# Wide tile products moved between the narrow products of the rest, in a cluster attention and expert kernel

## The chip, the cores and the metric

The kernel runs on one core of one Trainium2 chip. The metric is the device time of one execution in microseconds. A core has TensorE (PE, matrix products into PSUM; its weight loads are shown apart as PEld), VectorE (DVE), ScalarE (ACT), GpSimd (POOL) and SyncE (SP, which issues most transfers). Each engine runs its own instruction stream in order and waits for the others by semaphores.

## The reference

Attention in which a query sees only the keys of its own cluster feeds a layer of 16 experts; every token goes to one expert, chosen by an argmax over 4 groups and then over 4 experts of the group.

```
mask   = argmax(q_n @ c_n)[:, :, :, None] == argmax(k_n @ c_n)[:, :, None, :]
attn   = softmax(where(mask, q @ k.T / 8, -1e9));  x = (attn @ v).reshape(3072, 512)
for g in range(4):
    for e in range(4):                      # tokens whose argmax is (g, e)
        h  = maximum(x[tok] @ w1[g, e], 0)  # w1: 512 x 1024
        ye = h @ w2[g, e]                   # w2: 1024 x 512
        out[tok] = (g_w * e_w)[:, None] * ye
```

Shapes: q, k, v are 4 x 8 x 768 x 64 in fp32, with 16 clusters a head.

## The kernel before

The first 400 us or so are the attention; the change leaves them as they are. Then the experts run, one after another. Each fp32 operand is split into a high and a low fp16 part, so that a product becomes three: high by high, low weights by high, high weights by low.

One expert (that with most tokens) is done first. The other 15 are sorted by their counts into ranks 0 to 14. Rank k has room for a fixed number of tokens, `caps[k]`: 288, 272, 256, 240, 232, 224, 216, 208, 200, 192, 184, 176, 168, 160, 160. A rank has a first product (x by w1, 96 matmuls: 8 blocks of 128 hidden features, 12 matmuls each) and a second product (h by w2). The second product has three forms:

- by tile: 128 tokens are the stationary operand and 512 output features stream past; 24 wide matmuls per tile of 128 tokens, and the tile is ready to be written out;
- turned (features by tokens, `all_features`, L1724): w2 is the stationary operand and the tokens stream past, 96 matmuls as wide as the tokens; the result is evicted as two fp16 parts (yh on ACT, yl on DVE), and `settle` (L1358) turns it back with 8 small products a tile;
- both: the first 128 tokens by tile (`tile_then`, L1714), the rest (`caps[k]` - 128 tokens: 112 down to 48) turned (`rest_first`, L1697). The function `both` decides it by column counts: ranks 3 to 11 take this form, ranks 12 to 14 are wholly turned, ranks 0 and 1 too, by the older function `down`; rank 2 goes by tile, also through `down`.

From rank 2 on, `phases` (L1604) writes the order out by hand. One turn k of its loop does, on PE: the first product of rank k; the transposes of the tokens of rank k+1; the second product of rank k-1, which for the form `both` is all 96 narrow matmuls of the rest, then `settle` of what rank k-2 owes, then the 24 wide ones of the tile. Between them `fills` puts pieces of the weight stream: each piece is one of 8 quarters (512 KB in fp32) of a rank's weights, loaded by SP, its high part made by ACT or POOL (the second argument of `fills` says which) and its low part by DVE (L1060). Six loads are under way at a time; a load waits for the DVE instruction that frees a staging buffer.

`sized` (L1585) wraps blocks of 12 matmuls in a branch: PE reads the rank's count, and takes a body that is 24 columns narrower if the count allows it (the first matmul of a block stays at full width). Both bodies stand in PE's program behind each other. Every product is pinned to the order as written.

PSUM has a pool of two banks for second products (psy), one of two banks for the small ones (psm), and four banks for first products (psh three, and one called psm, from the pool `fourth`). `emit` (L1370) scales a finished tile on ACT into one of three y buffers (L1372), and POOL scatters it to the output (L1374).

Of the kernel before, what the change touches and what calls it, by code (L numbers as in the profile page):

```python
# [13 lines left out]
F32 = mybir.dt.float32  # L14
# [8 lines left out]
P = 128  # L23
# [967 lines left out]
class Experts:  # L991
# [6 lines left out]
    short, eng = (), None  # L998
    AHEAD = 6
    SLT = 14  # L1000
    FILL, SETTLE, TOK = (0, 1, 2, 3, 4, 5, 6, 7), 2, 5
    HI = (0, 1, 0, 1, 0, 1, 0, 1)
    LEAD = 12
# [353 lines left out]
    def settle(self):  # L1357

        nc = self.nc
        while self.owed:  # L1360
            ys, M, gcols, idcols = self.owed.pop(0)
            for t, (g, idc) in enumerate(zip(gcols, idcols)):
                n = min(P, M - t * P)
                py = self.R.psm.tile([P, 512], F32, name="psm")
                for d in range(self.R.KD):
                    for i, y in enumerate(ys):
                        nc.tensor.matmul(out=py[:, d * P:(d + 1) * P], lhsT=y[:, d * M + t * P:d * M + (t + 1) * P], rhs=self.back, start=i == 0, stop=i == 1)
                self.emit(py, n, g, idc)
# [233 lines left out]
    def phases(self, first, xT, down, bg):  # L1602

        nc, tc, R, E = self.nc, self.tc, self.R, self.R.E  # L1604
        KD, FC, D = R.KD, self.F // P, self.D
        xgs = self.gathers(first + 1)
        _, self.counts = nc.values_load_multi_w_load_instructions(self.ei[0:1, E:2 * E - 1], engines=[ET.PE], skip_runtime_bounds_check_because="they are only compared with constants")
        R.psm = self.psm2
        h = None

        self.pinned, self.behind_of = (nc.cur_bb, len(nc.cur_bb.bb.instructions)), {}

        def fills(n, eng):
            self.eng = eng
            for _ in range(n):
                next(self.fill, None)

        for k in range(first, E):
            if k < E - 1:
                M = self.caps[k]  # L1620
                while self.ready < 4 * k + 4:
                    fills(1, 0)
                w1h, w1l = self.weights_of(k, 0)
                hp = [next(self.quads).tile([P, 512], F32, name="psh" if i < 3 else "psm").rearrange("p (a x) -> p a x", a=2) for i in range(4)]

                prods = [(w, x, c) for c in range(KD) for w, x in ((w1h, 0), (w1h, 1), (w1l, 0))]
                for f in range(FC):

                    def up(m):
                        for i, (w, x, c) in enumerate(prods):  # L1630
                            n = m if i else M
                            self.mm = nc.tensor.matmul(out=hp[f // 2][:, f % 2, 0:n], lhsT=w[:, c, f * P:(f + 1) * P], rhs=xT[:, x, c, 0:n], start=i == 0, stop=i == len(prods) - 1)  # L1632

                    self.sized(k, (24,), up)
                nh = [self.xp.tile([P, FC, M], F16, name=f"h{x}") for x in "hl"]
                for j, p in enumerate(hp):
                    fs = slice(2 * j, 2 * j + 2)
                    nc.scalar.activation(out=nh[0][:, fs], in_=p[:, :, 0:M], func=AF.Relu)  # L1638
                    nc.vector.scalar_tensor_tensor(out=nh[1][:, fs], in0=p[:, :, 0:M], scalar=0.0, in1=nh[0][:, fs], op0=ALU.max, op1=ALU.subtract)
            fills(2, 1)  # L1640
            if k < E - 2:
                nT = self.xp.tile([P, 2, KD, self.caps[k + 1]], F16, name="xT")
                for t, xg in enumerate(xgs):
                    self.transposed(nT, xg, t, min(P, nT.shape[3] - t * P), R.psm.tile([P, 512], F32, name="psm"), nc.scalar.copy)
                xgs = self.gathers(k + 2) if k < E - 3 else None
            fills(2, 0)
            while self.ready2 < 4 * (k - 1) + 4:
                fills(1, 0)
            m = self.caps[k - 1]
            due, self.owed = self.owed, []  # L1650
            if h is None or not (self.both(m) or self.feature_major(m)):
                down = down if h is None else self.down(h, m, self.weights_of(k - 1, 1), *self.columns_of(k - 1))
                for i, _ in enumerate(down):
                    if i == 1:
                        new, self.owed = self.owed, due
                        self.settle()
                        self.owed = new
                    if i in (2, 4, 6):
                        fills(1, i == 4)
                fills(1, 0)  # L1660
                next(bg, None)
            else:
                (self.rest_first if self.both(m) else self.all_features)(k - 1, m, h)
                fills(2, 1)
                if k == E - 2:
                    nc.gpsimd.drain()  # L1666
                new, self.owed = self.owed, due
                self.settle()
                self.owed = new
                fills(2, 0)  # L1670
                next(bg, None)
                if self.both(m):
                    self.tile_then(k - 1, h)
            if k < E - 1:
                h, xT = nh, nT if k < E - 2 else None
        for _ in self.fill:
            pass
        self.settle()
        self.pin()
# [12 lines left out]
    def products(self, h, W):  # L1692
        return [(w, a, f) for w, a in ((W[0], h[0]), (W[1], h[0]), (W[0], h[1])) for f in range(self.F // P)]

    def rest_first(self, k, M, h):

        nc, KD, n = self.nc, self.R.KD, M - P  # L1697
        prods = self.products(h, self.weights_of(k, 1))
        pr = self.ps_y.tile([P, 512], F32, name="psy")[:, 0:KD * n].rearrange("p (d m) -> p d m", m=n)

        for d in range(KD):
            for i, (w, a, f) in enumerate(prods):
                self.mm = nc.tensor.matmul(out=pr[:, d], lhsT=w[:, f, d * P:(d + 1) * P], rhs=a[:, f, P:M], start=i == 0, stop=i == len(prods) - 1)
        ys = [self.xp.tile([P, (KD - 1) * n + P], F16, name=f"y{x}") for x in "hl"]
        if n < P:
            for y in ys:
                nc.vector.memset(y[:, KD * n:], 0.0)
        yh, yl = (y[:, 0:KD * n].rearrange("p (d m) -> p d m", m=n) for y in ys)
        nc.scalar.activation(out=yh, in_=pr, func=AF.Copy, scale=1.0 / YS)
        self.ev = nc.vector.scalar_tensor_tensor(out=yl, in0=pr, scalar=1.0 / YS, in1=yh, op0=ALU.mult, op1=ALU.subtract)  # L1710
        g, ids = self.columns_of(k)
        self.owed.append((ys, n, g[1:], ids[1:]))

    def tile_then(self, k, h):  # L1714

        nc, D = self.nc, self.D
        prods = self.products(h, self.weights_of(k, 1))
        pt = self.ps_y.tile([P, 512], F32, name="psy")
        for i, (w, a, f) in enumerate(prods):
            self.mm = nc.tensor.matmul(out=pt, lhsT=a[:, f, 0:P], rhs=w[:, f], start=i == 0, stop=i == len(prods) - 1)  # L1720
        g, ids = self.columns_of(k)
        self.emit(pt, P, g[0], ids[0])

    def all_features(self, k, M, h):  # L1724

        nc, KD = self.nc, self.R.KD
        prods = self.products(h, self.weights_of(k, 1))
# [6 lines left out]
        for c in range(2):  # L1734
            py = self.ps_y.tile([P, 512], F32, name="psy").rearrange("p (a x) -> p a x", a=2)

            for j in range(2):
                d = 2 * c + j
# [10 lines left out]
            nc.scalar.activation(out=yh[:, ds], in_=py[:, :, 0:M], func=AF.Copy, scale=1.0 / YS)  # L1749
            self.ev = nc.vector.scalar_tensor_tensor(out=yl[:, ds], in0=py[:, :, 0:M], scalar=1.0 / YS, in1=yh[:, ds], op0=ALU.mult, op1=ALU.subtract)  # L1750
        self.owed.append((ys, M, *self.columns_of(k)))

    def rest(self):
        self.again = True
# [99 lines left out]
def tile_cluster_attention_moe(ctx, tc, qT, kT, vr, cen, wr, w1, w2, out):  # L1854
# [39 lines left out]
    for i, _ in enumerate(ga):  # L1894
        with tc.issue_after(X.mm.ins):
            if i == X.SLT:
                X.xTB = X.tokens([X.xB], P)
# [45 lines left out]
```

## Time and profile before

| | us |
|---|---|
| median of 3 runs (729.63 to 731.92) | 731.0 |
| the profiled execution | 729.34 |
| its span, first to last instruction | 727.3 |
| PE busy in the span | 698.2 (96%) |
| DVE, POOL, ACT busy | 585.7, 504.4, 487.8 |
| mean granted clock of PE, share of full speed | 0.993 |

The 2.0 us between the execution's time and its span lie outside of the first and the last instruction. A PE row's duration is longer than the distance from one matmul's start to the next, since matmuls overlap; the distance between starts is what a matmul costs in a stream. Idle time before a row stands in brackets with what ended it; "issue" means that the profile shows nothing that the engine waited for. DMA share is the mean busy share of the 16 DMA engines; queue q8 carries instructions.

### The profile page before, as it was taken

Reading aid. Unit: us, or ns where it says so; the run is one execution under the profiler, and the core shown is the slowest. Engines: PE = TensorE matmul, PEld = TensorE weight load, DVE = VectorE, ACT = ScalarE, POOL = GpSimd, SP = SyncE. Lnnn points to the kernel's source line nnn. Section 1 sums busy time; section 2 is a strip of 40 time slices with the busy share of each in tenths; the row PEclk is TensorE's granted clock in tenths of the full one; section 3 lists DMA queues with packets and bytes.
Section 4 is the critical chain, followed back from the end, with each engine's and each line's share of the span. In section 5 each row is a group of like instructions: output and inputs, shape, how many; then the busy total and the mean of one; then the engine's idle time right before and its main releaser. Section 6 shows DMA issues by size and latency. Waiting matters only on the chain. (4 is left out here: it accounts for less than half of the span.)

```text
span 727.3 us, 22864 instructions
## 1 busy us (share of the span) xinstructions
PE 698.2 (96%) x9035; PEld 578.8 (80%) x9035; DVE 585.7 (81%) x1202; ACT 487.8 (67%) x932; POOL 504.4 (69%) x522
## 2 busy tenths in 40 slices
PE   8899999999999999999999999999999999999984
PEld 4677888888888888888888877898788888877884
DVE  6898989899898998998888677556599798788742
ACT  6669987888878978787888366354445554565422
POOL 8799999897898988979896454313645444667433
PEclk9999999999999999999999999999999999999998
DMA  8735634516255262340430698626778776888721
GB/s 242 208 108 170 190 106 133 172 47 188 66 140 179 64 174 58 79 132 2 148 100 14 223 379 292 205 86 220 255 256 311 280 274 238 308 291 301 252 90 51
DMA packets 45813, 127.93 MB, mean 176 GB/s; under 512 B 7648, under 2 KB 12640, under 8 KB 45688
## 3 DMA queue, kind: packets, MB, share of 16 engines
q1 hardware_dynamic: 40668, 112.64, 48.1%
q0 software_dynamic: 4864, 13.54, 5.2%
q8 instruction: 85, 1.39, 0.8%
q14 instruction: 40, 0.33, 0.1%
q10 hardware_dynamic: 156, 0.03, 0.0%
HBM read 93.30 MB, written 13.54 MB: 147 GB/s over the span
## 5 line engine op out<-in xcount | busy, mean ns | idle before, releaser
L436 POOL TENSOR_TENSOR pl<-p 128x512 f16<-128x512 f32 x278 | 284.6, 1044 | 46.8 <-ACT p L434 43.5
L390 DVE TENSOR_REDUCE mpart<-psc 128x1 f32<-128x512 f32 (+1 forms) x282 | 190.5, 684 | 23.4 <-PE psc L387 22.2
L434 ACT ACTIVATE p<-psf 128x512 f32<-128x512 f32 x288 | 170.7, 599 | 39.6 <-PE psf L430 34.3
L454 PE MATMUL pso<-V,pl 128*128 128x129 f16 x1152 | 165.1, 219 | 0.8 <-POOL pl L436 0.8
L454 PE MATMUL pso<-V,p 128*128 128x129 f16 x1152 | 165.6, 219 | 0.0
L429 PE MATMUL psf<-A 82*128 82x384 f16 (+2 forms) x576 | 142.6, 273 | 3.1 <-ACT p L434 2.3
L430 PE MATMUL psf<-B 128*128 128x384 f16 (+2 forms) x576 | 143.4, 273 | 0.0
L454 PEld LDWEIGHTS <-pl 128*128 128x128 f16 x1152 | 112.0, 97 | 21.9 <-POOL pl L436 1.3
L1374 POOL DMA_INDIRECT out_dram<-y,ri x33 | 44.1, 1335 | 113.1 <-ACT y L1373 106.5
L454 PEld LDWEIGHTS <-p 128*128 128x128 bf16 x1152 | 112.2, 97 | 8.5
L387 PE MATMUL psc<-A 80*128 80x512 f16 (+1 forms) x376 | 106.6, 325 | 0.9 <-DVE A L335 0.5
L430 PEld LDWEIGHTS <-B 128*128 128x128 f16 x576 | 56.5, 98 | 14.7 <-issue 5.5
L429 PEld LDWEIGHTS <-A 82*128 82x128 f16 x576 | 56.0, 98 | 9.6 <-issue 1.1
L1638 ACT ACTIVATE hh<-psh 128x320 f16<-128x320 f32 (+11 forms) x39 | 19.7, 506 | 45.0 <-PE psh L1632 45.0
L1060 DVE SCALAR_TENSOR_TENSOR wl1b<-st,wh1b 128x1024 f16<-128x1024 f32 x32 | 44.6, 1425 | 3.2 <-ACT wh1b L1057 1.7
L1060 DVE SCALAR_TENSOR_TENSOR wl0a<-st,wh0a 128x1024 f16<-128x1024 f32 x32 | 41.1, 1310 | 4.9 <-ACT wh0a L1057 4.9
L1057 ACT ACTIVATE wh0a<-st 128x1024 f16<-128x1024 f32 x30 | 31.1, 1059 | 20.3 <-DMA st<-w 17.5
L1060 DVE SCALAR_TENSOR_TENSOR wl1a<-st,wh1a 128x1024 f16<-128x1024 f32 x28 | 37.3, 1363 | 8.9 <-POOL wh1a L1059 7.2
L387 PEld LDWEIGHTS <-A 80*128 80x128 f16 x384 | 36.2, 98 | 9.7 <-issue 0.8
L1234 POOL DMA_INDIRECT xg<-xbuf,ri x25 | 29.5, 1181 | 19.0 <-DVE rg L1389 8.8
L1632 PEld LDWEIGHTS <-wh0a 128*128 128x128 f16 x448 | 39.1, 98 | 4.2 <-issue 2.9
L1059 POOL TENSOR_SCALAR wh1a<-st 128x1024 f16<-128x1024 f32 x25 | 32.2, 1303 | 14.0 <-DMA st<-w 12.2
(455 smaller groups left out, 1699.7 us busy)
## 6 DMA issues: line engine op xcount, KB each, us to landing
st<-w SPq DMA_DIRECT2D x128, 512.0 KB
B<-parts SPq DMA_DIRECT2D x60, 192.0 KB
kx<-kT SPq DMA_DIRECT2D x16, 384.0 KB
qx<-qT SPq DMA_DIRECT2D x16, 384.0 KB
vx<-vr SPq DMA_DIRECT2D x16, 384.0 KB
xbuf<-xs SPq DMA_DIRECT2D x4, 1536.0 KB
A<-parts SPq DMA_DIRECT2D x30, 192.0 KB
A<-mk SPq DMA_DIRECT2D x56, 24.0 KB
```

The lines of the kernel that those rows point to most:

```text
L387: last["mm"] = nc.tensor.matmul(out=pc[:, off:off + k1 - k0], lhsT=QA[h % 8][0:80, c * P:(c + 1) * P], rhs=KA[h % 8][0:80, k0:k1], start=T ...
L390: nc.vector.tensor_reduce(out=(mp[:, 0, 0:1], mp[:, :, 1], mp[:, 1, 0:1])[i], in_=pc.rearrange("p (a x) -> p a x", a=n), axis=AX.X, op=ALU ...
L429: nc.tensor.matmul(out=o, lhsT=KA[h % 8][0:82, ks], rhs=QA[h % 8][0:82, q0:q1], start=True, stop=False)
L430: nc.tensor.matmul(out=o, lhsT=KBs[h][:, ks], rhs=QBs[h][:, q0:q1], start=False, stop=True)
L434: exps[9 * h + u] = cfg["exp"] = nc.scalar.activation(out=p32, in_=pf, func=AF.Exp, scale=QK / (SQ * SQ))
L436: lo = (nc.vector if u in (EARLY if h < 2 else DVE_LO[h % 8] if h < NH - 2 else DVE_END) else nc.gpsimd).tensor_tensor(out=pl, in0=p32, in ...
L454: nc.tensor.matmul(out=o, lhsT=p[:, bs], rhs=vv, start=c == 0 and q % HB == 0 and i == 0, stop=c == NCH - 1 and i == 1, skip_group_check=True)
L1057: nc.scalar.activation(out=h, in_=st, func=AF.Copy, scale=WS)
L1059: nc.gpsimd.tensor_scalar(out=h, in0=st, scalar1=WS, scalar2=0.0, op0=ALU.mult, op1=ALU.add)
L1060: nc.vector.scalar_tensor_tensor(out=l, in0=st, scalar=WS, in1=h, op0=ALU.mult, op1=ALU.subtract)
L1374: d = nc.gpsimd.indirect_dma_start(out=self.out, out_offset=bass.IndirectOffsetOnAxis(ap=idc, axis=0), in_=y[0:n], in_offset=None, bounds_ ...
L1632: self.mm = nc.tensor.matmul(out=hp[f // 2][:, f % 2, 0:n], lhsT=w[:, c, f * P:(f + 1) * P], rhs=xT[:, x, c, 0:n], start=i == 0, stop=i == ...
```

## The change

Rank for rank: in the form `both`, the wide products of the tile no longer follow the rest; a generator (`tile_products`) hands them out, and six stand behind each of the rest's four parts of 24. In turns 10 to 12, whose first products are at most 184 tokens wide (`MIX`), 24 of the tile's products, now in two halves of 256 columns, stand in the first product instead, four behind each of the blocks 2 to 7; the other 24 stand between the rest's parts. `settle` stands behind the rest's second part, the rest's eviction (`rest_out`) behind its last, and the last two `fills` of a turn behind the tile's `emit`.

Rank 14 goes from the turned form to the new order (three wide products behind each part, six more ahead of `settle`, six behind it), and its rest takes a psh bank. Rank 2 goes from the tile form to `all_features`. Ranks 12 and 13 stay turned. The first products of ranks 13 and 14 lose their branches and run at 160 columns. In `settle`, a third tile takes the bank of `fourth`.

```diff
+    MIX = 184
...
-                py = self.R.psm.tile([P, 512], F32, name="psm")
+                py = (self.fourth if t == 2 and self.R.psm is self.psm2 else self.R.psm).tile([P, 512], F32, name="psm")
...
+                mix = None
+                if h is not None and self.caps[k] <= self.MIX and self.both(self.caps[k - 1]):
+                    mix = self.tile_products(k - 1, h)
+                    next(mix)
                 for f in range(FC):
...
-                    self.sized(k, (24,), up)
+                    self.sized(k, (24,) if k < E - 3 else (), up)
+                    if mix is not None and f > 1:
+                        self.some(mix, 4)
...
-            if h is None or not (self.both(m) or self.feature_major(m)):
-                down = down if h is None else self.down(h, m, self.weights_of(k - 1, 1), *self.columns_of(k - 1))
+            if h is None:
...
-            else:
-                (self.rest_first if self.both(m) else self.all_features)(k - 1, m, h)
+            elif k < E - 1 and not self.both(m):
+                self.all_features(k - 1, m, h)
                 fills(2, 1)
...
-                if self.both(m):
-                    self.tile_then(k - 1, h)
+            else:
+                if k == E - 1 or mix is None:
+                    mix = self.tile_products(k - 1, h)
+                    next(mix)
+                pr, rest = self.rest_products(k - 1, m, h)
+                for d in range(KD):
+                    for _ in range(2 * KD * 3):
+                        next(rest)
+                    if d == 1:
+                        fills(2, 1)
+                        new, self.owed = self.owed, due
+                        self.settle()
+                        self.owed = new
+                    self.some(mix, 3 if k == E - 1 else 6)
+                self.rest_out(k - 1, m, pr)
+                if k == E - 1:
+                    self.some(mix, 6)
+                    self.settle()
+                for _ in mix:
+                    pass
+                fills(2, 0)
+                next(bg, None)
...
+    def tile_products(self, k, h):
+        nc, D = self.nc, self.D
+        prods = self.products(h, self.weights_of(k, 1))
+        pt = self.ps_y.tile([P, 512], F32, name="psy")
+        yield
+        halves = 2 if k + 1 < self.R.E - 1 and self.caps[k + 1] <= self.MIX else 1
+        for c in range(halves):
+            cs = slice(c * D // halves, (c + 1) * D // halves)
+            for i, (w, a, f) in enumerate(prods):
+                self.mm = nc.tensor.matmul(out=pt[:, cs], lhsT=a[:, f, 0:P], rhs=w[:, f, cs], start=i == 0, stop=i == len(prods) - 1)
+                yield
+        g, ids = self.columns_of(k)
+        self.emit(pt, P, g[0], ids[0])
```

On PE, in the second product of rank 4 (104 tokens of rest; narrow products have w2 as weights and end in 104, wide ones have hh as weights and end in 512). Before:

```order
L1703 MATMUL psy<-hl,wh1b 128x104
L1367 LDWEIGHTS yh
L1367 MATMUL psm<-back,yh 128x128
...
L1367 LDWEIGHTS yl
L1367 MATMUL psm<-back,yl 128x128
L1720 LDWEIGHTS hh
L1720 MATMUL psy<-wh1b,hh 128x512
L1720 LDWEIGHTS hh
L1720 MATMUL psy<-wh1b,hh 128x512
```

And in the changed kernel, at the end of the first of the rest's four parts:

```order
L1734 MATMUL psy<-hl,wh1b 128x104
L1791 LDWEIGHTS hh
L1791 MATMUL psy<-wh1b,hh 128x512
...
L1791 LDWEIGHTS hh
L1791 MATMUL psy<-wh1b,hh 128x512
L1734 LDWEIGHTS wh1b
L1734 MATMUL psy<-hh,wh1b 128x104
```

The 96 narrow products that stood in one row are now four rows of 24, with six wide ones behind each.

On ACT, around the second product of rank 7 (yh is the eviction of its rest, y from psm the tile that `settle` turned back, y from psy the wide tile, wh0b the high part of two weight quarters). Before:

```order
L1709 ACTIVATE yh<-psy 128x352
L1373 ACTIVATE y<-psm,rg 96x512
L1057 ACTIVATE wh0b<-st 128x2x512 x2
L1597 UNCONDITIONAL_BRANCH
L1373 ACTIVATE y<-psy,rg 128x512
L1597 UNCONDITIONAL_BRANCH x4
L1638 ACTIVATE hh<-psh 128x400
```

And in the changed kernel:

```order
L1374 ACTIVATE y<-psm,rg 96x512
L1747 ACTIVATE yh<-psy 128x352
L1598 UNCONDITIONAL_BRANCH
L1374 ACTIVATE y<-psy,rg 128x512
L1058 ACTIVATE wh0b<-st 128x2x512 x2
L1598 UNCONDITIONAL_BRANCH x4
L1645 ACTIVATE hh<-psh 128x400
```

The two weight quarters stood ahead of the wide tile's y, and stand behind it now; the eviction of the rest stands behind the y of `settle`.

On ACT, the last tiles of the program (from the y of rank 12's second tile). Before:

```order
L1373 ACTIVATE y<-psm,rg 40x512
L1597 UNCONDITIONAL_BRANCH x5
L1749 ACTIVATE yh<-psy 128x320
L1597 UNCONDITIONAL_BRANCH x2
L1749 ACTIVATE yh<-psy 128x320
L1373 ACTIVATE y<-psm,rg 128x512
L1373 ACTIVATE y<-psm,rg 32x512
L1373 ACTIVATE y<-psm,rg 128x512
L1373 ACTIVATE y<-psm,rg 32x512
```

And in the changed kernel:

```order
L1374 ACTIVATE y<-psm,rg 40x512
L1374 ACTIVATE y<-psm,rg 128x512
L1374 ACTIVATE y<-psm,rg 32x512
L1747 ACTIVATE yh<-psh 128x128
L1374 ACTIVATE y<-psm,rg 32x512
L1374 ACTIVATE y<-psy,rg 128x512
```

Four tiles stood in one row at the end; now two of them (rank 13) stand ahead of the eviction of rank 14's rest, and two (rank 14) behind it.

## Rows read from the trace of the kernel before

**Rows 1.** The page: the span, and the queue that carries instructions (packets, MB, share).
```profile
span 727.3 us, 22864 instructions
q8 instruction: 85, 1.39, 0.8%
```
**Rows 2.** Waits of PE, 640 to 728 us (us in total, times, longest).
```profile
PE psy L1703 <- issue: 2.8, 2, 1.7
PE psm L1632 <- issue: 2.8, 2, 2.2
```
**Rows 3.** Timeline of PE around stalls (start, us, instruction, idle before).
```profile
582.78 0.40 PE L1249 MATMUL psm<-ident,xg 128*128 128x128 f16 x4 [0.42 <-PE psm L1632]
...
602.20 0.27 PE L1703 MATMUL psy<-hl,wh1a 128*128 128x80 f16 x3 [0.39 <-issue]
...
621.73 0.29 PE L1703 MATMUL psy<-hh,wl1b 128*128 128x72 f16 x4 [0.50 <-issue]
...
668.71 0.23 PE L1703 MATMUL psy<-hh,wh1a 128*128 128x48 f16 x3
670.68 0.28 PE L1703 MATMUL psy<-hh,wh1a 128*128 128x48 f16 x5 [1.74 <-issue]
...
698.72 0.29 PE L1632 MATMUL psm<-xT,wh0a 128*128 128x160 f16 x2 [2.18 <-issue]
```
**Rows 4.** Busy time in stretches: four from a chunk's boundary on (clock, DMA share, GB/s last).
```profile
635.20:636.17 0.97, 0.97 (x29) 0.97 (x27) 0.19 (x1) 0.70 (x2) 0.00 (x0) 1.00 1.04 401
665.33:668.32 2.99, 2.99 (x76) 2.99 (x74) 1.30 (x3) 1.73 (x3) 1.81 (x3) 1.00 1.01 390
692.63:696.20 3.57, 3.57 (x63) 3.54 (x61) 3.30 (x5) 1.20 (x3) 2.94 (x3) 1.00 0.95 296
698.72:708.40 9.68, 9.68 (x120) 9.68 (x121) 3.37 (x6) 0.88 (x2) 0.47 (x1) 0.82 0.02 5
```
**Rows 5.** DMA queues in 696.1 to 697.2 us.
```profile
q8 instruction: 1, 0.02, 5.4%
```
**Rows 6.** Busy time in stretches: first product, 24 wide products, two turned ranks.
```profile
472.07:481.68 9.61, 9.61 (x97) 9.40 (x98) 2.53 (x4) 2.00 (x4) 0.00 (x0) 1.00 0.01 3
655.59:660.77 5.18, 5.18 (x28) 2.35 (x26) 5.18 (x7) 2.90 (x4) 4.40 (x3) 1.00 0.89 327
700.41:708.44 8.03, 8.03 (x98) 8.03 (x97) 3.37 (x6) 0.88 (x2) 0.00 (x0) 0.82 0.02 4
```
**Rows 7.** Timeline of PE, narrow products of rank 11's rest.
```profile
667.50 0.36 PE L1703 MATMUL psy<-hh,wh1a 128*128 128x48 f16 x8
667.70 0.36 PE L1703 MATMUL psy<-hh,wl1a 128*128 128x48 f16 x8
```
**Rows 8.** Waits of PE, 470 to 520 us.
```profile
PE psm L1367 <- ACT y L1373: 0.9, 2, 0.5
```
**Rows 9.** Timeline of ACT and POOL at the end.
```profile
715.75 1.25 ACT L1373 ACTIVATE y<-psm,rg 128x512 f32<-128x512 f32 x2
721.79 0.68 ACT L1373 ACTIVATE y<-psm,rg 32x512 f32<-32x512 f32 x1 [3.92 <-PEq L1811]
...
710.10 1.51 POOL L1374 DMA_INDIRECT out_dram<-y,ri  x1 [10.92 <-ACT y L1373]
...
716.72 1.01 POOL L1374 DMA_INDIRECT out_dram<-y,ri  x1 [3.86 <-ACT y L1373]
...
722.74 0.89 POOL L1374 DMA_INDIRECT out_dram<-y,ri  x1 [2.52 <-ACT y L1373]
```
**Rows 10.** Weights: timeline of DVE and PE at rank 14, and SP's longest wait after 560 us.
```profile
689.27 2.35 DVE L1060 SCALAR_TENSOR_TENSOR wl0a<-st,wh0a 128x1024 f16<-128x1024 f32 x2
...
692.02 0.29 PE L1632 MATMUL psh<-xT,wh0a 128*128 128x160 f16 x2
...
SPq L1050 <- DVE wl1b L1060: 38.8, 16, 10.2
```

More of the change, by code (lines that the diff above doesn't have):

```diff
@@ L1693, in products, with some, rest_products, each @@
         return [(w, a, f) for w, a in ((W[0], h[0]), (W[1], h[0]), (W[0], h[1])) for f in range(self.F // P)]
-    def rest_first(self, k, M, h):
-        nc, KD, n = self.nc, self.R.KD, M - P
[L1698 to L1703, printed above, removed]
+    def some(self, products, n):
+        for _ in range(n):
+            next(products, None)
+    def rest_products(self, k, M, h):
+        KD, n = self.R.KD, M - P
+        pr = (self.ps_y.tile([P, 512], F32, name="psy") if k < self.R.E - 2 else next(self.quads).tile([P, 512], F32, name="psh"))[:, 0:KD * n].rearrange("p (d m) -> p d m", m=n)
+        prods = self.products(h, self.weights_of(k, 1))
+        def each():
+            for d in range(KD):
+                for i, (w, a, f) in enumerate(prods):
+                    self.mm = self.nc.tensor.matmul(out=pr[:, d], lhsT=w[:, f, d * P:(d + 1) * P], rhs=a[:, f, P:M], start=i == 0, stop=i == len(prods) - 1)
+                    yield
+        return pr, each()
+    def rest_out(self, k, M, pr):
+        nc, KD, n = self.nc, self.R.KD, M - P
         ys = [self.xp.tile([P, (KD - 1) * n + P], F16, name=f"y{x}") for x in "hl"]
@@ L1712, in rest_first @@
         self.owed.append((ys, n, g[1:], ids[1:]))
[L1714 to L1722, printed above, removed]
     def all_features(self, k, M, h):
@@ L1751, in all_features @@
         self.owed.append((ys, M, *self.columns_of(k)))
+    def tile_products(self, k, h):
+        nc, D = self.nc, self.D
+        prods = self.products(h, self.weights_of(k, 1))
+        pt = self.ps_y.tile([P, 512], F32, name="psy")
[3 more added lines that the diff above has]
+            cs = slice(c * D // halves, (c + 1) * D // halves)
+            for i, (w, a, f) in enumerate(prods):
+                self.mm = nc.tensor.matmul(out=pt[:, cs], lhsT=a[:, f, 0:P], rhs=w[:, f, cs], start=i == 0, stop=i == len(prods) - 1)
+                yield
+        g, ids = self.columns_of(k)
+        self.emit(pt, P, g[0], ids[0])
     def rest(self):
```

## The prediction

> **What bounds the kernel now.** I read the page first, then the busy time in stretches, then PE's waits and its timeline, and last the ends of ACT and POOL. The page says that PE is 96% busy, and no other engine is above 81%. So what counts is where PE stands still. Behind 640 us it waits 5.6 us in four stalls whose releaser is "issue" [rows 2], and three shorter ones lie ahead of that (0.42, 0.39, 0.50 us) [rows 3]: 6.9 us in seven stalls. Three lie at a jump between two bodies of a first product or behind its last body; the other four lie in the middle of a row of narrow products, where no operand is new.
>
> What they share is their place in the program. Counted in PE's instruction order, without the jump at the end of each second body (it leads to the next row), the seven stand 768, 768, 1280, 768, 512 and 768 instructions apart, all multiples of 256. The instruction queue moves 1.39 MB in 85 packets, 16 KB each [rows 1]. I take one packet for a chunk of 256 instructions. In the 698.72 us stall one such packet lies just ahead of the release [rows 5]: narrowing the window gives a start at 696.20, a landing at 697.14, and PE goes on at 698.72. In the stall before 670.68 the same numbers are 668.32, 669.26 and 670.68. So PE goes on some 1.4 to 1.6 us behind the landing, and the packet itself starts late: PE passed the chunk's boundary before at 692.63 and 665.33, 3.57 and 2.99 us earlier, while the DMA share was 0.95 and 1.01 with weights [rows 4]. With a DMA share of 0.02 [rows 4] there is no such delay and no stall. Under load 21 such delays lie between 0.72 and 3.57 us, mean 1.9 (one of 0.97 and the two longest are in [rows 4]). My reading: a chunk must last longer than delay + 0.95 + 1.45 us, or PE runs dry. Narrow products cost 25 ns each (8 in 0.20 us) [rows 7], wide ones 216 ns (24 in 5.18 us) [rows 6], so a chunk that holds only narrow ones, or bodies of which half is jumped over, lasts least: without their stalls, the seven chunks last 3.4 to 4.8 us.
>
> The clock: rank 13's 96 turned products take 8.03 us at a mean granted clock of 0.82 [rows 6], that is part of them at the 1.2 GHz level. Ahead of this PE had stood for 2.18 us [rows 3], and since 640 us for 1.74 and, in two stalls, 1.7 more (5.6 less the two [rows 2, 3]).
>
> **The change part by part.** I follow PE to the end of rank 13's turned products (708.44 us in before [rows 6]; call it T), then the tail.
>
> *Stalls.* I laid the changed program's order out with the durations above and cut it each 256 instructions. From 560 us on the chunks last 5.0 to 5.7 us or 7 to 9 us, with three exceptions (4.8, 4.6, and 4.0 us at rank 12's turned products, which stay as they are). With the 21 delays of before, a chunk of 5.2 us stalls one time in four, by 0.3 us, and one of 4.0 us every second time, by 1.1 us. Summed over the chunks 1.6 us stay: 6.9 - 1.6 = 5.3 us gained. Bounds: 6.9 (none stays) and 0 (the delay grows with the load that a faster PE makes). I take 5.3, near the upper row, since only a few chunks stay below 5 us.
>
> The Trainium skill (Runtime: NRT & Kernel Launch, Instruction fetch mechanics) says that instructions come in blocks of 256 by the sequencer's own DMA queue, that this is mostly hidden, and that a taken branch out of the window forces a fetch. The trace agrees on the 256, not on hidden. By the part on branches only the stalls at the bodies would go; that is the first rival.
>
> *Clock.* Without a stall of 2 us ahead of it I expect rank 13's products at full clock: 8.03 x (1 - 0.82) = 1.4 us gained. Bounds 0 and 1.4.
>
> *Settle.* The third tile waits twice for an eviction of ACT, 0.9 us in all [rows 8]; with the bank of `fourth`, whose first product DVE has read by then, that goes: 0.9 us.
>
> *Added columns.* Rank 14's first product at 160 columns instead of 136 (its count lies under 136, so the narrower body ran): 88 matmuls x 24 columns at 2.4 GHz are 0.9 us more. A body's branch costs 0.03 us (9.61 us for rank 2's first product [rows 6], 22,464 columns are 9.36; the rest over 8 branches): 16 fewer, 0.5 us less. Rank 2: 48 wide products (10.4 us) become 96 of 232 columns with 8 branches and 16 back products of 56 ns: 10.5 us. The halves of 256 columns add 72 matmuls with some 2.5 ns each, 0.2 us. Together +0.7 us. That wide and narrow products alternate costs nothing by itself where the kernel already alternates two products; not shown for these shapes, so between 0 and a branch's 0.03 us for each of some 110 changes, 3.3 us. I take 0, since such alternation of before shows no gap.
>
> T becomes 708.4 - 5.3 - 1.4 - 0.9 + 0.7 = 701.5.
>
> *Tail.* In before four tiles come in one row at the end, with three y buffers: the last one's eviction starts at 721.79, 5.07 us behind the scatter of the third before it (716.72) [rows 9]. The row names a branch of PE's sequencer as releaser, which writes nothing that this eviction reads, so I take the buffer. From T the execution's span lasts 18.9 us. Changed, from T: 16 back products 0.9, four parts of 24 narrow ones at 25 ns 2.4, rank 13's 16 back products 0.9, 24 wide ones 5.2, 8 back products 0.45: 9.9 us, where before had 9.0. Rank 13's first scatter goes out at T + 4.7 and frees its buffer at T + 9.8, ahead of the last tile's need (T + 10.3). The eviction of rank 13's second tile waits for rank 12's first scatter (710.10 [rows 9], T + 1.7 + 5.1 = T + 6.8), then rank 14's rest is evicted by T + 8.1, just when PE wants it. Last eviction 0.68, 0.27 to the scatter, and from the scatter's start to the end 4.56 (722.74 to 727.3): T + 15.8. That is 3.1 us gained; bounds 0 (another wait for a buffer) and 4.
>
> *Weights.* The last two quarters of a turn now stand behind the wide tile's y on ACT, 3 to 4 us later for ranks 4 to 9, and the loads that wait for DVE's low parts (SP's longest wait [rows 10]) with them. They belong to the rank after next, so nothing on PE asks for them at once. The smallest reserve is at rank 14: DVE ends the low part at 691.62, PE's blocks that need it come 2.6 us behind the start at 692.02 [rows 10], 3.0 us. Taken as 0; without that cover, up to 2 us in the last ranks.
>
> Span: 701.5 + 15.8 = 717.3; with the 2.0 us outside 719.3, against 729.34 of the profiled execution: 10.0 us, 1.4%. The median of before is 1.7 us above this execution; set off from it, 721.0.
>
> **The rivals.** (1) Only branches count. Then the four stalls in straight code stay (0.39 + 0.50 + 2.8 us) with that at 582.78, and 2.8 of the 6.9 us go: 721.0 + 2.5 = 723.5. For it: the longest stall lies at a jump. Against: the spacing, and four stalls without any jump. (2) The stalls stay, since the packets wait longer the fuller the DMA engines are; clock and tail as before except for the tail's buffer: 721.0 + 5.3 + 1.4 = 727.7. For it: DMA shares of 0.95 to 1.01. Against: chunks are 1 to 2 us longer. (3) Weights take over in part: PE, 8 us ahead, meets DVE's low parts, and half of stalls and clock is given back: 724.4. (4) Slower: two quarters of each turn start 3 to 4 us later on ACT, SP's loads follow, and PE waits for weights in each of the 9 turns with the form `both`. From 1.35 us a turn on (12.2 us, the gain and 2.2 more) the kernel is slower; at 1.5 us it is 734.5. Against: reserves of 3 us at rank 14.
>
> **How the numbers follow.** Forecast 0.62 (its own range 717 to 724), rival 1 0.11, rival 2 0.11, rival 3 0.10, rival 4 0.06. About 0.3% (2.2 us) is what can be told from no change: faster means below 728.8. Forecast, rivals 1 and 3 are faster, rival 2 two times in five not: faster 0.87, same 0.07, slower 0.06. The range goes from 715.0 (no stall stays, the tail gains 4) to 727.5.
>
> **What would show it.** Right: no "issue" stall above 1 us on PE behind 560 us, those left at the same spacing of 256; granted clock 1.00 in rank 13's turned products; the last eviction on ACT no longer waits 3.9 us; T near 701.5. Wrong: PE waits for wh or wl (weights), or stalls of the same sum at new places.

## The result and the profile after

The changed kernel takes 723.4 us (median of 5 runs, 720.8 to 725.2), the kernel before 731.5 us beside it (5 runs, 729.6 to 733.1): ratio 0.990, 95% interval 0.9874 to 0.9926. The forecast was 721.0 us. Of the same changed kernel a second set of runs gave 722.45 us, ratio 0.990 (0.9868 to 0.9934).

The span of its profiled execution is 721.6 us against 727.3 [rows 1]. I split both at two places that can be found in either trace: the first product of rank 2 starts (472.07 us before, 474.61 after), and rank 13's turned products end (T: 708.44 before, 703.41 after).

| us | before | after | difference | forecast |
|---|---|---|---|---|
| start to rank 2 | 472.07 | 474.61 | +2.54 | 0 |
| rank 2 to T | 236.37 | 228.80 | -7.57 | -6.9 |
| T to the end | 18.86 | 18.16 | -0.70 | -3.1 |

So the middle did a little more than was forecast, the tail a quarter of it, and the front, which the change does not touch, came out longer. First PE's waits behind 470 us, as [rows 2] shows them of before: what waited, on which engine and line, for what; the sum in us, how often, and the longest.

```profile
PE psm L1250 <- PE psm L1637: 0.4, 1, 0.4
PE psy L1734 <- issue: 0.3, 1, 0.3
PE psh L1637 <- issue: 0.2, 1, 0.2
PE psh L1734 <- issue: 0.2, 1, 0.2
PE psy L1791 <- issue: 0.2, 1, 0.2
```

That is all that PE waits for. The third row is the stop at rank 2's start, which is as long in the kernel before. The other four rows and one stop of 0.13 us that the list leaves out are 1.2 us in five short stops behind 560 us, where seven stalls took 6.9 us [rows 2, 3]. No row names wh or wl, so PE never waits for weights, and none names an eviction of ACT, so the waits of `settle` [rows 8] are gone. (The first row's releaser is PE itself; it is a stop at a multiple of 256 instructions, like the others ahead of T. The fourth row, 0.24 us, lies behind T and not at such a place; ahead of T 1.05 us are left, with one of 0.10 us.) Then the busy time in two stretches: start and end, length, each engine's busy time with its instructions, PE's granted clock as a share of full speed, DMA share, GB/s.

```profile
474.61:703.41 228.80, 227.68 (x3114) 205.91 (x3114) 184.90 (x229) 112.42 (x168) 147.30 (x98) 1.00 0.73 251
696.77:703.41 6.64, 6.64 (x100) 6.64 (x97) 3.36 (x6) 0.87 (x2) 0.00 (x1) 1.00 0.02 5
```

PE is idle for 1.1 us between rank 2 and T. The second row is the 96 turned products of rank 13 (its counts take in a few neighbours that overlap): 6.64 us at clock 1.00, where [rows 6] has 8.03 us at 0.82. Now the tail on ACT and on POOL (start, duration, engine and line, operation, out<-in and shape; in brackets the idle time before it and what ended it):

```profile
710.75 0.68 ACT L1374 ACTIVATE y<-psm,rg 32x512 f32<-32x512 f32 x1 [3.22 <-DMA out_dram<-y,ri]
711.34 0.25 ACT L1747 ACTIVATE yh<-psh 128x128 f16<-128x128 f32 x1
712.62 0.68 ACT L1374 ACTIVATE y<-psm,rg 32x512 f32<-32x512 f32 x1 [1.03 <-issue]
713.91 0.69 ACT L1374 ACTIVATE y<-psy,rg 128x512 f32<-128x512 f32 x1 [0.62 <-PE psy L1791]
...
713.57 0.88 POOL L1375 DMA_INDIRECT out_dram<-y,ri  x1 [0.98 <-ACT y L1374]
714.88 0.99 POOL L1375 DMA_INDIRECT out_dram<-y,ri  x1 [0.42 <-ACT y L1374]
```

The last eviction now waits for the last products and not 3.9 us for a buffer [rows 9], and the last scatter starts at T + 11.47. But this scatter has 128 rows, and from its start to the end 6.69 us go by. In [rows 9] the last one, of 32 rows, took 4.56.

### The profile page after: what moved, and what is told of

Same layout as the page of the kernel before. It is cut to its first block, busy times and chain, and to the rows that moved or that the text cites. A ratio compares the mean times of both kernels' runs of the same rounds, so it can differ in the third digit from the quotient of the medians.

```text
span 721.6 us, 23145 instructions
## 1 busy us (share of the span) xinstructions
PE 699.7 (97%) x9187; PEld 588.9 (82%) x9187; DVE 588.6 (82%) x1203; ACT 484.7 (67%) x932; POOL 531.9 (74%) x523
## 3 DMA queue, kind: packets, MB, share of 16 engines
q8 instruction: 85, 1.39, 0.8%
## 4 chain that ended last, share of the span: by engine, by line
PE 80%; ACT 7%; DVE 5%; POOL 4%; issue 3%; DVEq 0%; ACTq 0%; POOLq 0%
PE pso L454 13%; PE psh L1637 10%; PE psy L1791 7%; PE psf L429 7%; PE psf L430 7%; PE psc L387 6%; PE psy L1734 4%; PE psh L1278 4%; PE psm L1637 3%; PE psy L1326 3%; PE psy L1773 3%; POOL pl L436 3%; ACT p L434 3%; PE psm L1368 1%; DVE mpart L390 1%
## 5 line engine op out<-in xcount | busy, mean ns | idle before, releaser
L1375 POOL DMA_INDIRECT out_dram<-y,ri x33 | 46.2, 1401 | 58.5 <-ACT y L1374 50.2
L1060 POOL TENSOR_SCALAR wh1a<-st 128x1024 f16<-128x1024 f32 x26 | 41.6, 1611 | 21.4 <-DMA st<-w 15.4
L1235 POOL DMA_INDIRECT xg<-xbuf,ri x25 | 35.5, 1421 | 22.5 <-PE psm L1250 9.2
L1061 DVE SCALAR_TENSOR_TENSOR wl0a<-st,wh0a 128x1024 f16<-128x1024 f32 x32 | 46.0, 1461 | 5.1 <-ACT wh0a L1058 2.8
L1061 DVE SCALAR_TENSOR_TENSOR wl0b<-st,wh0b 128x1024 f16<-128x1024 f32 x28 | 43.5, 1584 | 4.1 <-ACT wh0b L1058 4.1
L1061 DVE SCALAR_TENSOR_TENSOR wl1b<-st,wh1b 128x1024 f16<-128x1024 f32 x32 | 39.2, 1255 | 7.8 <-POOL wh1b L1060 6.0
L1645 ACT ACTIVATE hh<-psh 128x320 f16<-128x320 f32 (+11 forms) x39 | 19.5, 502 | 36.7 <-PE psh L1637 36.7
L1060 POOL TENSOR_SCALAR wh1b<-st 128x1024 f16<-128x1024 f32 x27 | 40.3, 1502 | 5.2 <-DVE wl1b L1061 2.3
L1637 PE MATMUL psh<-xT,wh0a 128*128 128x160 f16 (+10 forms) x336 | 41.2, 243 | 0.4 <-issue 0.2
```

The lines of the kernel that those rows point to most:

```text
L1060: nc.gpsimd.tensor_scalar(out=h, in0=st, scalar1=WS, scalar2=0.0, op0=ALU.mult, op1=ALU.add)
L1061: nc.vector.scalar_tensor_tensor(out=l, in0=st, scalar=WS, in1=h, op0=ALU.mult, op1=ALU.subtract)
L1375: d = nc.gpsimd.indirect_dma_start(out=self.out, out_offset=bass.IndirectOffsetOnAxis(ap=idc, axis=0), in_=y[0:n], in_offset=None, bounds_ ...
```

## The experiments

A word on counting: the chunks are counted as in the prediction, in PE's program order without the jump at the end of each second body, in units of 256 instructions. T is always the end of rank 13's turned products.

**The kernel before, once more.** Does the pattern of stalls belong to the program or to one execution?

> The kernel before, unchanged. Theory: the seven stalls of its first profile come from the order of its code, so they stand at the same multiples of 256 instructions, each within 1 us of its size, 5 to 9 us in all; the small stalls at 414 to 420 us, seen in all profiles but the first of this kernel, differ from run to run and may be there. Rival: the stalls are an accident of the one profile, and others or none are seen. Time 728 to 733 in both cases.

One run, 733.85 us, span 731.8. PE's waits behind 470 us:

```profile
PE psy L1703 <- issue: 3.5, 3, 2.0
PE psm L1632 <- issue: 2.0, 2, 1.2
PE psm L1367 <- ACT y L1373: 1.2, 3, 0.5
PE psm L1249 <- ACT hh L1638: 1.0, 1, 1.0
PE psm L1249 <- PE psm L1632: 0.7, 1, 0.7
PE psh L1632 <- issue: 0.2, 1, 0.2
```

Seven stalls again, 0.4 to 2.0 us, 7.1 us in all. Six stand at the same points of the program, at the ends of chunks 60, 63, 71, 74, 76 and 79; the seventh is at 68 in place of 66. Two rows name ACT or PE as releaser, but these stops lie at the same boundaries; the name is what happened to end last. Single sizes differ by more than I had allowed (that at chunk 79 was 2.18 in the first profile, 0.75 here), the sum hardly. The small stalls ahead of 420 us, which the first profile of this kernel had not, are there:

```profile
PE psy L1300 <- issue: 1.6, 4, 0.5
PE psy L1309 <- issue: 0.3, 2, 0.2
```

The changed kernel has 2.0 us of the same at the same two places. Rank 2 starts at 476.32 us in this run of the kernel before, later than in the changed kernel (474.61). So the +2.54 us of the front is not the change's.

**Shift the program.** 32 small matmuls ahead of `phases`, that is 64 more instructions on PE and nothing else.

```diff
+        shift = R.psm.tile([P, 512], F32, name="psm")
+        for _ in range(32):
+            nc.tensor.matmul(out=shift[:, 0:8], lhsT=self.back, rhs=self.back[:, 0:8], start=True, stop=True)
```

> The kernel before, with 64 instructions (32 weight loads and 32 matmuls of 8 columns, about 0.8 us of PE) put ahead of the first product of rank 2; nothing else moves. Theory (a chunk of 256 PE instructions comes by a late packet): the stalls keep their spacing of multiples of 256 and all move 64 instructions towards the program's start, so none is left at the seven old places; their sum may change (3 to 9 us), since other chunks become the short ones. Rival (stalls belong to branches, or to what PE reads there): the stalls stay at the old instructions, 6.9 us in seven.

Span 731.5 us (one run, 733.6 us).

```profile
PE psh L1635 <- issue: 3.0, 2, 2.0
PE psy L1706 <- issue: 2.9, 3, 2.0
PE psm L1249 <- issue: 2.2, 2, 1.5
PE psm L1367 <- ACT y L1373: 1.2, 3, 0.5
```

2.0 us of the first row is a wait at the head of `phases`, which was there before too, but with 0.2 us. The six stalls behind 560 us stand at multiples of 256 of the longer program (chunks 63, 66, 69, 71, 74, 79; five of these numbers as in the first profile of before), 6.1 us in all, each therefore at code that lies 64 instructions earlier. None stayed with its old code, not even one that had stood at a jump. What counts is the place in the program. This is the run that speaks most plainly against the first rival.

**Half the bytes of each weight load.** Each load behind the attention moves one half of its 512 KB, and the splits read this half twice; half of the weights are left out of the computation.

```diff
-        nc.sync.dma_start(out=st.rearrange("p r c -> p (r c)"), in_=we[:, q])
+        n = 512 if self.stage2 else 1024
+        nc.sync.dma_start(out=st.rearrange("p r c -> p (r c)")[:, 0:n], in_=we[:, q][:, 0:n])
...
+        if self.stage2:
+            r = st.shape[1] // 2
+            st = st[:, 0:r].unsqueeze(1).broadcast_to([P, 2, r, st.shape[2]])
+            h, l = (w.rearrange("p (t r) c -> p t r c", t=2) for w in (h, l))
```

> The kernel before, but each weight load behind the attention moves only half of its bytes and the splits read this half twice (half of the weights are left out of the result). Theory (the packet waits behind weight transfers): the delay from a chunk's boundary to its packet shrinks, most stalls go, at most 2 us of the 6.9 stay, the clock stays full in rank 13's turned products, and the time falls by 5 to 9 us. Rival (PE's stalls come from branches or from reading the program itself, whatever else the DMA engines do): the stalls stay at 5 to 7 us.

Span 724.1 us (one run, 726.2 us). The waits:

```profile
PE psm L1372 <- ACT y L1378: 1.2, 3, 0.5
PE psy L1708 <- issue: 0.6, 2, 0.3
PE psh L1637 <- issue: 0.2, 1, 0.2
```

And the stretch from 560 to 700 us, with the columns as above:

```profile
560.00:700.00 140.00, 139.28 (x2021) 118.35 (x2020) 115.90 (x145) 72.44 (x107) 82.44 (x66) 1.00 0.53 161
```

PE's code is the one of before, with its short chunks, but at a DMA share of 0.53 (before: 0.78 in the same stretch) the packets start on the mean 0.5 us behind the boundary and never more than 1.9, where before had 1.5 and 3.6 (those that start ahead of it counted as 0). Behind 560 us 0.6 us of stalls is left of 6.9. The time fell by 4.4 us against the kernel before beside it (730.6), where I had expected 5 to 9: rank 2 started 5.2 us later, behind more of the small stalls ahead of 420 us (3.4 us). So both halves of the reading hold: a packet that starts late behind weights, and a chunk too short to cover it.

**Only the spread.** The kernel before with six wide products behind each quarter of the rest in ranks 3 to 11, all else as before (the new functions are those of the change).

```diff
+    MIX = 0
...
-            else:
-                (self.rest_first if self.both(m) else self.all_features)(k - 1, m, h)
+            elif not self.both(m):
+                self.all_features(k - 1, m, h)
```

> Of the change only this: in ranks 3 to 11 six wide tile products stand behind each quarter of the rest (settle, eviction and fills as in the change); no wide products in first products, ranks 2 and 14 in their old forms, all branches and the bank of settle as before. Theory: the four stalls in the rests (3.7 us) go down to 1 us at most, the three at first products (3.2 us, with the clock's 1.4) may stay: 727 us, 2 to 4 us faster. Rival (only branches count): nothing changes, 731.

725.4 us, ratio 0.992 (0.9892 to 0.9951): 5.1 us less than the kernel before beside it (730.6), more than the 2 to 4 us that I had expected.

```profile
PE psy L1774 <- issue: 1.8, 1, 1.8
PE psm L1368 <- ACT y L1374: 1.2, 3, 0.5
PE psy L1735 <- issue: 0.8, 1, 0.8
PE psm L1637 <- issue: 0.6, 1, 0.6
```

3.1 us of stalls are left of 6.9, and the longest, 1.8 us, is in rank 12's turned products, which stay as they were. The 2.18 us stall ahead of rank 13's turned products did not come, and these run at clock 1.00; I had allowed for both to stay.

**Only the one width.** The first products of ranks 13 and 14 without branches, all else as before.

```diff
-                    self.sized(k, (24,), up)
+                    self.sized(k, (24,) if k < E - 3 else (), up)
```

> Of the change only this: the first products of ranks 13 and 14 have one width and no branches. Theory: the two stalls there (2.8 us) and the half clock in rank 13's turned products (1.4 us) go, 0.5 us comes in columns: 727.5, 3 to 4 us faster; the stalls in the rests stay. Rival (only branches count): the same gain. Rival (stalls come whatever the order): 732, slower by the columns.

729.3 us, ratio 0.997 (0.995 to 0.999): a small gain, 1 to 2 us where I had expected 3 to 4. The waits:

```profile
PE psy L1703 <- issue: 3.9, 3, 1.8
PE psm L1249 <- ACT hh L1638: 1.5, 1, 1.5
PE psm L1367 <- ACT y L1373: 1.2, 3, 0.5
```

Two stretches, the one with the last of the long stalls and the one behind it:

```profile
671.00:674.00 3.00, 1.19 (x48) 1.10 (x45) 3.00 (x3) 1.91 (x3) 2.35 (x3) 1.00 0.68 210
674.06:677.48 3.42, 3.42 (x23) 1.84 (x20) 3.42 (x6) 1.96 (x3) 1.30 (x2) 0.50 0.69 217
```

The last two first products have no stall, those in the rests stay, in straight code without any jump. But one of 1.5 us is new and one of 1.1 us grew to 1.65, so that 5.4 us of stalls are left of 6.9. The drop of the clock is seen here in its own place: PE stood for 1.8 us within the first stretch, and the second stretch, 3.4 us that begin 1.1 us behind the stall's end, runs at 0.50, the 1.2 GHz level, on rank 11's wide products.

**The changed kernel again, and without one of its parts.** These stand beside a repeat of the changed kernel.

> The changed kernel once more, beside the parts of it that follow. Small PE stalls at 414 to 420 us, in code that the change leaves alone, were in its first profile (2.5 us) and not in that of before. If they differ from run to run: time 723 to 724, and the front part may come out with or without them. If they belong to the changed kernel: there again, with 2 to 3 us.

722.45 us, ratio 0.990 (0.9868 to 0.9934), span 719.6, 0.4 us of stalls behind 560 us (0.13 of it ahead of T), rank 2 to T in 226.9 us. The small stalls of the front are there with 1.8 us. The spread between two profiles of one kernel, 1.9 us in this stretch, is as large as several of the terms that I had weighed.

Without wide products in first products:

```diff
-    MIX = 184
+    MIX = 0
```

> The changed kernel without wide products in first products (all 24 of a tile stand between the rest's parts in every turn). Theory, chunks of 256 instructions: ranks 9 to 12 have the narrowest products, and their chunks get short again where only first and turned products follow each other; as in the run that only spread, stalls of 1.5 to 2 us come back behind 680 us: 725.0. Rival, only jumps cost: nothing changes, or 0.2 us less since the halves' added matmuls go: 723.2.

723.6 us, ratio 0.989 (0.9866 to 0.9912). I had expected 725.0, and this failed: stalls of 1.4 us ahead of T, much as in the changed kernel (three more stops, 1.2 us, lie behind T). That part of the change makes no difference that can be seen.

With the branches kept in the last two first products:

```diff
-                    self.sized(k, (24,) if k < E - 3 else (), up)
+                    self.sized(k, (24,), up)
```

> The changed kernel with the branches kept in the last two first products. Arithmetic without stalls: 0.9 us less for rank 14's narrower columns, 0.5 us more for the branches: 723.0. Theory, chunks: half of each body is jumped over, so those chunks last shorter, and one or two stalls of 1 to 2 us come back between 670 and 697 us: 724.5 to 726. Rival, jumps themselves cost: the same time, but the stall ends right at a jump and not at a multiple of 256 instructions; that is what the place has to tell.

725.25 us, ratio 0.992 (0.989 to 0.9945), 2.8 us over the changed kernel beside it, though the two intervals overlap. The three stops between 680 us and T:

```profile
687.20 0.95 PE L1773 MATMUL psy<-hh,wl1b 128*128 128x144 f16 x8 [1.51 <-issue]
692.80 0.29 PE L1637 MATMUL psh<-xT,wh0a 128*128 128x136 f16 x2 [1.28 <-issue]
697.17 0.29 PE L1637 MATMUL psm<-xT,wh0a 128*128 128x136 f16 x2 [0.41 <-issue]
```

They lie exactly 256 instructions apart, each between two neighbouring matmuls. The first is in rank 12's turned products, and the other two are within a body, not at its jump (the `x2` behind the bracket are the rest of it). So a branch costs here by what it jumps over: code that fills a chunk and takes no time.

**Rank 14 turned as before.**

```diff
-            elif k < E - 1 and not self.both(m):
+            elif not self.both(m):
```

> The changed kernel with rank 14 wholly turned again, as before, so that the order in the rows up to T is that of the changed kernel and the tail is that of before. Theory (the tail of the change gained only some 0.7 us, since its last scatter now has 128 rows): the tail takes 18.9 us again behind T, and the time is some 0.7 us more than the changed kernel's: 723 to 724.5. Rival (the step as predicted, 3.1 us gained by the tail): 726.5.

723.3 us, ratio 0.990 (0.9878 to 0.993), span 719.9, T 701.14, and 18.77 us from there to the end. The last eviction and the last scatter:

```profile
713.97 0.68 ACT L1374 ACTIVATE y<-psm,rg 32x512 f32<-32x512 f32 x1 [3.40 <-DMA out_dram<-y,ri]
...
714.92 0.89 POOL L1375 DMA_INDIRECT out_dram<-y,ri  x1 [2.01 <-ACT y L1374]
```

The wait for the buffer is back (here the trace names the scatter itself), and the last scatter starts at T + 13.78, 2.3 us later than in the changed kernel. But it has 32 rows, and the end comes 4.98 us behind its start and not 6.69. The two nearly cancel. The rival, 726.5, is out.

**The last tile ahead of the rest.** In the last turn of the changed kernel, wide products 8 and 16 behind the rest's first and second part (those with low weights last), `settle` of rank 13 behind the first part, and other buffers for the last turn's tiles.

```diff
-                    if d == 1:
+                    if d == (0 if k == E - 1 else 1):
...
-                    self.some(mix, 3 if k == E - 1 else 6)
+                    self.some(mix, (8, 17, 0, 0)[d] if k == E - 1 else 6)
                 self.rest_out(k - 1, m, pr)
-                if k == E - 1:
-                    self.some(mix, 6)
-                    self.settle()
...
+        if k + 1 == self.R.E - 1:
+            prods = prods[0:8] + prods[16:24] + prods[8:16]
```

> The changed kernel with another order in the last turn: the 24 wide products stand behind the rest's first (8) and second part (16), the ones with low weights last, settle of rank 13 behind the first part, so that the tile of 128 rows is scattered ahead of the 32 rows of the rest, and the last turn's tiles use five other buffers. Theory, a scatter of 128 rows needs 6.7 us to the end and one of 32 rows 4.6: the end comes at T + 16.7 in place of T + 18.2, 721.9. Rival, the time behind the last scatter's start is the same for both sizes and what counts is when PE is done: the last scatter starts at T + 12.2, later than now, and the time is 723.4 or more.

722.4 us, ratio 0.987 (0.9841 to 0.9895), T 705.45, end 722.54: a tail of 17.09 us. Its last two scatters:

```profile
714.79 0.98 POOL L1375 DMA_INDIRECT out_dram<-xg,ri  x1 [2.42 <-ACT xg L1374]
717.61 0.89 POOL L1375 DMA_INDIRECT out_dram<-xg,ri  x1 [1.83 <-ACT xg L1374]
```

The first has 128 rows, the last 32; it starts at T + 12.16, later than in the changed kernel, and yet the end comes 1.1 us earlier, 4.93 us behind it. That is the theory's sign and two thirds of its size. Up to T the order is that of the changed kernel, and yet 2.5 us of stalls stand there, the longest of them:

```profile
PE psy L1791 <- issue: 1.2, 1, 1.2
```

So the same code leaves very different sums from one execution to the next. The same order once more:

> The order with the last tile ahead of the rest once more, to see whether it is faster than the changed kernel. Its tail was 17.1 us in one profile, against 18.2 and 18.7 in two profiles of the changed kernel, so 1.1 to 1.6 us less: 721.5, ratio to before 0.988. Rival (what the last turn gains is lost in other waits): 723, ratio 0.990.

721.35 us, ratio 0.989 (0.9864 to 0.9922), tail 17.17 us, stalls of 0.8 us ahead of T. Both profiles have the shorter tail; in the time, this order and the changed kernel can't be told apart.

**What is left without the two parts that showed nothing.** The changed kernel with `MIX = 0` and rank 14 turned (the two edits above together).

> The changed kernel without two of its parts: no wide products in first products, and rank 14 wholly turned. What stays is six wide products behind each quarter of the rest, one width in the last two first products, rank 2 turned, and the third tile's bank. Each of the two parts taken alone made no difference that could be measured. Theory (they carry nothing, the spread and the one width carry the gain): ratio to before 0.990, 723.5, stalls behind 560 us 1 to 2 us. Rival (each covers for the other, as the run that only spread had a 1.8 us stall in rank 12): 726.

723.7 us, ratio 0.992 (0.9893 to 0.9949), stalls of 1.9 us ahead of T (three, of which 1.1 the longest). The time stands with the theory, the ratio between the two; since its interval holds 0.990 as well, it is not shown whether the two parts bring 1 us together or nothing.

## Why the prediction came out as it did

**What bounds the kernel.** Right. Up to T PE's standstills counted, with the half clock behind one of them, and the shift, the repeat and the halved loads show what they are: places at multiples of 256 instructions, and packets that start late behind weights. The time alone would not have told it: my first rival (only branches count) gave 723.5 us, and 723.4 was measured. It is the traces that rule it out. The 0.39 + 0.50 + 2.8 us in straight code, which it kept, went; and in the shifted program no stall stayed at its jump. The Trainium skill (Runtime: NRT & Kernel Launch, Instruction fetch mechanics) holds that the fetch by blocks is mostly hidden, and that a taken branch to a place out of the window forces a fetch; these runs agree on the block of 256 and disagree on hidden, with 6.9 and 7.1 us in seven stalls of two executions.

**Stalls.** Right in kind; that the size fits is in part luck. 1.6 us were to stay, and ahead of T 1.05 us did. In the three other profiles with the same order up to T (the repeat and the two with the tile ahead) it was 0.1, 2.5 and 0.8 us. This is not because packets come sooner: between 560 and 700 us they start on the mean 1.7 us behind the boundary, longest 3.6 (before 1.5 and 3.6). The chunks last longer: counted without their stalls, four between 560 us and T are under 5 us, the shortest 4.15, where before had fourteen, the shortest 3.6. (Counted so, the seven stalled chunks of before last 3.6 to 5.0 us, and not 3.4 to 4.8.) The 1.45 us from a landing to where PE goes on fit the changed kernel's stops too (1.45 to 1.6); two boundaries were passed without a stop 1.2 and 1.4 us behind a landing. That a lucky place of the boundaries made the gain is not likely: the shift gave the old order new boundaries and kept 6.1 us, while each order with wide products spread in the rests has boundaries of its own, and they left 0.1 to 3.1 us, with the branches kept 4.1.

**Clock.** 1.4 us forecast, 8.03 - 6.64 = 1.39 measured. That the drop follows a standstill is shown three times beside this: in the run with one width it stands behind the 1.8 us stall at 671 us, in the shifted program behind the 2.0 us stall at 674 us (half clock from 677.5 to 680.9), and in the repeat of before, behind its 2.0 us stall at 674 us, the stretch that follows has 0.65 (below). Not every stall brings it: the clock stayed at 1.00 behind the 1.74 us of [rows 3], the 1.8 us in the run with only the spread, and the 2.0 us at the head of `phases` in the shifted program.

```profile
676.27:681.00 4.73, 4.73 (x62) 3.54 (x62) 4.73 (x7) 2.16 (x4) 3.04 (x3) 0.65 0.88 315
```

**Settle and added columns.** The waits for ACT's y, 0.9 us by [rows 8], are gone; where the old bank is used they are in each profile with 1.2 us. The +0.7 us for columns, halves and branches was not measured by itself. With it the sum closes: -5.9 (6.95 to 1.05) - 1.4 - 0.9 + 0.7 = -7.5, measured -7.57.

**Tail.** Here the prediction failed. The 4.56 us "from the scatter's start to the end" were those of a scatter of 32 rows, and the change puts one of 128 rows last. The start was right, T + 11.24 forecast and T + 11.47 measured; the term itself was 6.69 us, 2.1 more. Over all profiles, the ten whose last scatter has 32 rows took 4.5 to 5.1 us, the four with 128 rows 5.7 to 7.3. The packets of the last scatter, before and after (packets, MB, share of the DMA engines in windows of 0.6 and 2.4 us around them):

```profile
q0 software_dynamic: 32, 0.01, 6.8%
...
q0 software_dynamic: 80, 0.26, 31.7%
```

The first packet goes out 1.5 us behind the scatter's start in both, and from the last packet to the end it is 2.7 and 3.0 us. What differs is the time in which the packets go out, 0.4 us against 2.2 (1.2 to 2.8 in the four profiles). So the price goes by what a scatter sends: 10 KB before (at 2 KB a row, no more than 5 of the 32 rows) and 262 KB after. The whole tail took 18.7 to 19.5 us in the eight profiles with rank 14 turned, 18.2 to 18.7 in four of the changed order, 17.1 and 17.2 with the tile ahead. So of 3.1 us some 0.7 came (0.5 between the means, 19.0 and 18.5), and turning rank 14 back loses nothing that can be measured. The row that I took the price from shows no shape; the shape stands in the row of ACT that feeds it, and that I did not read.

**Front, and the way to the median.** I had set the code ahead of rank 2 at no difference, and added 1.7 us because the profiled execution of before lay that far under its median. The profiles show why these hang together, though it is not proven: that execution is the only one in which the small stalls ahead of 420 us are missing, and the repeat with them took 733.85 us. So the profile of after has 2.5 us that the first one of before lacks, and needs no allowance for the median. T at 703.41 against 701.5 forecast (+1.9) and the tail (+2.4) make the span 4.3 us longer than forecast; without the allowance 2.4 us of this are left in the median, 723.4 against 721.0. All in all the two errors that count are a tail price and an execution that was taken for typical. The range's lower end was added up wrongly besides: no stall left (1.6 us) and 4 us from the tail (0.9 more) give 718.5, not 715.0.

**Rivals 2 to 4.** The stalls did not stay, and PE's waits have no row for weights; 227.68 of 228.80 us between rank 2 and T are busy.

## What to carry to other kernels

Stalls with the releaser "issue" under heavy DMA traffic should be laid against the instruction count of that engine first. If they stand at multiples of a block, what counts is how long a block lasts against how late the next one starts, and a jump counts by the code that it skips; long instructions spread among short ones remove most of them. And a transfer's price is taken from one of the same size that moves as much, above all for the last one of a kernel.

## What was not expected of the hardware

- Between 413 and 421 us, in 13 of 14 profiles, PE stops every few instructions for 0.1 to 1.2 us, 1.8 to 3.4 us in all, early in a chunk whose packet, by my count, had landed 9 us before the chunk began. The DMA share was 0.99 there in the changed kernel, and 1.01 in the one profile without. Three such stops, six to eight instructions apart, are in the last turn of two of these runs, and a single one (0.24 and 0.28 us) in that of the two profiles of the changed kernel. Behind those at 413 to 421 us five profiles show 3.4 us at half clock. What they are stays open.
- A scatter with four times the rows takes 1.6 us more from its start to the end of the execution (means 6.4 and 4.8 us); in bytes it moves 262 KB against 10 KB.
- 64 instructions more on PE let its first wait in `phases` grow from 0.2 to 2.0 us, in one run; I can't say why.
